# A shorter opening, row norms on VectorE, merged copies and stores from GpSimd in a spectral block with its gradients

## The chip, the cores and the metric

One core of one Trainium2 chip runs the whole program in one launch. Times are device microseconds (us), medians over several executions. TensorE does the matmuls, VectorE, ScalarE and GpSimd the elementwise work, and SyncE issues most transfers. A ratio below is the mean time of one kernel's fast runs over that of the other's of the same rounds, so it is not quite the ratio of the medians quoted beside it; under 1 is faster.

## The reference, cut to what matters

```python
mod = (silu(c) @ w_mod).reshape(1, 6, 1, -1)      # sa, ca, ga, sb, cb, gb
h = layernorm(x) * (1 + ca) + sa
x = x + ga * irfft2(rfft2(h) * (w_r + 1j * w_i))  # a 2-D filter over 2048 x 512
h = layernorm(x) * (1 + cb) + sb
x = x + gb * (relu(h @ w1 + b1)**2 @ w2 + b2)     # 512 -> 1792 -> 512
return x, gradients of all inputs for grad_out
```

The transforms are matmuls with tables of sines that the kernel computes on the chip. `grad_out @ w2^T` depends on no earlier result but the gate `gb`, so its 224 matmuls of 512 columns can be done at any time before the feed-forward part; the kernel uses them as **filler** for TensorE's gaps. Some names that follow: a *fold* adds and subtracts mirrored quarters of a row before it is transformed; the *condition* is c; *scale row* and *gate row* are the rows 1 + ca and gb of `mod`, and the *gate column* (gb2x) is twice gb, turned; psA, psB, psC, psG and the like are tiles in PSUM, TensorE's output memory.

## The kernel before

The filler is placed by a scheduler at low priority (`LATE`), wherever TensorE would otherwise stand:

```python
def back_products(b):                       # b: one of four blocks of 512 rows
    if b > 1:
        scale_g(b)                          # g * 2 gb, VectorE
    with Priority(tc, LATE):
        for fc in range(NFC):               # 14
            ps = mmps.tile([P, SB], FP32, name="mm")
            for dc in range(4):
                nc.tensor.matmul(ps, lhsT=w2T[...], rhs=gT[b][:, :, dc, :], ...)
            with tc.high_priority():
                if fc % 3 == 0:
                    nc.vector.tensor_copy(out=gaT[b][:, fc, :], in_=ps)
                else:
                    nc.scalar.copy(out=gaT[b][:, fc, :], in_=ps)
```

The filter (w_r, w_i) is loaded into eight tiles Z by GpSimd and stored at once, in padded form, for the backward pass; later the complex product of the forward pass overwrites Z in place:

```python
for gi in range(8):
    load_w(gi)                                       # GpSimd queue
    nc.sync.dma_start(wz_dram[:, gi], Z[gi])         # SyncE queue
...
def ew_f(gi, X):                                     # after row transform of group gi
    K["cmul"] = cmul(nc, ew, X, Z[gi], Z[gi][:, :, 0, 0:DF], Z[gi][:, :, 1, 0:DF], False)
    nc.sync.dma_start(xs_dram[:, gi], X)
```

## Time and profile before

| what | value |
|---|---|
| time, first three runs | 433.97 us (431.92 to 434.96) |
| TensorE busy | 398.7 us, 92% of the span |
| VectorE, ScalarE, GpSimd busy | 82%, 59%, 9% |
| last fold of the first stage ends | 40.4 us |
| products of the backward pass that accumulate for long ("gp products") begin | 157.2 us |

For comparing kernels whose stages shift, I cut the first 157 us of the kernel before anew, at events instead of round times: first transform matmul; start of the last fold; first matmul of the table products (psG); first copy of the inverse transform (Tsb); first feed-forward product; first gp product. The busy times of these stretches (columns: stretch, its length, then busy us and instructions of TensorE, weight loads, VectorE, ScalarE, GpSimd; then granted TensorE clock, DMA share, GB/s):

```profile
0.00:14.50 14.50, 4.44 (x14) 1.35 (x14) 9.72 (x54) 6.75 (x12) 9.83 (x54) 1.00 0.97 240
14.50:39.70 25.20, 22.84 (x120) 12.35 (x121) 23.11 (x62) 19.11 (x46) 13.33 (x28) 1.00 0.98 263
39.70:80.00 40.30, 38.02 (x265) 21.22 (x265) 32.33 (x108) 36.04 (x66) 17.62 (x31) 1.00 0.96 264
80.00:93.30 13.30, 13.27 (x121) 8.69 (x121) 10.60 (x20) 7.89 (x15) 0.00 (x0) 1.00 0.83 285
93.30:114.70 21.40, 19.51 (x125) 9.73 (x124) 18.50 (x44) 18.67 (x36) 0.00 (x0) 1.00 0.70 157
114.70:157.20 42.50, 41.29 (x187) 18.06 (x187) 31.43 (x65) 21.26 (x38) 0.00 (x0) 1.00 0.67 218
```

The difference of length and first busy figure in each line is TensorE's idle time: 10.1 us in the opening, 2.4 in A, 2.3 in tables and row transform (B), 0.0 in the table products (C), 1.9 in D, 1.2 in the feed-forward part. The sum is 17.8 us.

### The profile page before, as it was taken

Reading aid. Unit: us, or ns where it says so; the run is one execution under the profiler, and the core shown is the slowest. Engines: PE = TensorE matmul, PEld = TensorE weight load, DVE = VectorE, ACT = ScalarE, POOL = GpSimd, SP = SyncE. Lnnn points to the kernel's source line nnn. Section 1 sums busy time; section 2 is a strip of 40 time slices with the busy share of each in tenths; the row PEclk is TensorE's granted clock in tenths of the full one; section 3 lists DMA queues with packets and bytes.
Section 4 is the critical chain, followed back from the end, with each engine's and each line's share of the span. In section 5 each row is a group of like instructions: output and inputs, shape, how many; then the busy total and the mean of one; then the engine's idle time right before and its main releaser. Section 6 shows DMA issues by size and latency. Waiting matters only on the chain.

```text
span 432.7 us, 7098 instructions
## 1 busy us (share of the span) xinstructions
PE 398.7 (92%) x2353; PEld 196.1 (45%) x2375; DVE 353.7 (82%) x864; ACT 256.1 (59%) x487; POOL 40.9 (9%) x114
## 2 busy tenths in 40 slices
PE   2789999999899999999999999999999799995996
PEld 0344446654344444443444344455555464441332
DVE  6889768959995588969897998929577967989796
ACT  5578699679881286348536765465438374545231
POOL 7447930000000000000000000000000000000000
PEclk9999999999999999999999999999999999998899
DMA  9998899969595379779965997997995599999994
GB/s 237 222 293 278 223 282 273 318 222 188 177 360 191 121 127 329 186 162 226 276 189 158 210 330 271 245 244 217 263 300 160 166 245 257 255 257 255 247 246 137
DMA packets 147147, 101.11 MB, mean 234 GB/s; under 512 B 98945, under 2 KB 131590, under 8 KB 146726
## 3 DMA queue, kind: packets, MB, share of 16 engines
q1 hardware_dynamic: 145458, 98.01, 84.6%
q0 software_dynamic: 1088, 2.11, 2.1%
q10 hardware_dynamic: 564, 0.53, 0.4%
q8 instruction: 19, 0.31, 0.3%
q14 instruction: 18, 0.15, 0.1%
HBM read 35.44 MB, written 41.60 MB: 178 GB/s over the span
## 4 chain that ended last, share of the span: by engine, by line
PE 35%; DVE 25%; ACT 14%; DMA 12%; SPq 5%; issue 5%; POOL 2%; ACTq 0%; DVEq 0%
PE og L901 10%; PE mm L872 8%; PE mm L707 5%; PE mm L1173 4%; DMA out_dram<-gW 2%; PE psG L346 2%; ACT gab L712 2%; DVE gm_junk L470 2%; SPq L1168 2%; DMA n<-n_dram 2%; DMA out_dram<-gw 1%; DVE jk L1258 1%; ACT AE L329 1%; DMA y<-gx_dram 1%; DMA out_dram<-x 1%
## 5 line engine op out<-in xcount | busy, mean ns | idle before, releaser
L707 PE MATMUL mm<-gT,w2T 128*128 128x512 bf16 x224 | 57.8, 383 | 3.0 <-ACT gab L712 3.0
L1173 PE MATMUL mm<-g_sb,hn 128*128 128x512 bf16 x217 | 52.8, 394 | 3.3 <-DVE gw L1176 2.9
L872 PE MATMUL mm<-h2T,w 128*128 128x512 bf16 x224 | 53.4, 378 | 1.6 <-ACT r L874 1.4
L1104 PE MATMUL mm<-gab,h_sb 128*128 128x448 bf16 x256 | 51.4, 352 | 0.8 <-ACT gw L1108 0.8
L901 PE MATMUL og<-w1T,gab 128*128 128x512 bf16 x218 | 49.9, 379 | 1.0 <-DVE o L966 0.8
L901 PE MATMUL og<-w,h 128*128 128x512 bf16 x217 | 49.1, 379 | 0.3
L874 ACT ACTIVATE r<-mm,b1col 128x512 bf16<-128x512 f32 x56 | 37.0, 685 | 6.1 <-PE mm L872 3.3
L1173 PEld LDWEIGHTS <-hn 128*128 128x128 bf16 x224 | 21.6, 100 | 30.5 <-issue 8.2
L1104 PEld LDWEIGHTS <-h_sb 128*128 128x128 bf16 x256 | 24.6, 98 | 22.3 <-issue 1.7
L872 PEld LDWEIGHTS <-w 128*128 128x128 bf16 x224 | 21.1, 97 | 30.0 <-issue 8.3
L901 PEld LDWEIGHTS <-h 128*128 128x128 bf16 x224 | 21.8, 98 | 26.1 <-issue 0.9
L901 PEld LDWEIGHTS <-gab 128*128 128x128 bf16 x224 | 21.6, 98 | 25.9 <-issue 1.4
L707 PEld LDWEIGHTS <-w2T 128*128 128x128 bf16 x224 | 21.2, 98 | 22.4 <-issue 6.4
L914 ACT CAST G<-og 128x512 bf16<-128x512 f32 x16 | 9.2, 580 | 28.1 <-PE og L901 28.1
L876 DVE TENSOR_TENSOR h<-r 128x1024 bf16<-128x1024 bf16 x28 | 19.2, 687 | 4.8 <-ACT r L874 4.8
L1253 ACT ACTIVATE gs<-gn,inv 128x512 bf16<-128x512 bf16 x16 | 11.4, 716 | 18.6 <-DVE gn L1251 18.6
L712 ACT CAST gab<-mm 128x512 bf16<-128x512 f32 x36 | 21.4, 600 | 1.7 <-PE mm L707 1.5
L1108 ACT CAST gw<-mm 128x448 bf16<-128x448 f32 x16 | 8.7, 544 | 22.1 <-DMA out_dram<-gw 12.6
L418 DVE TENSOR_TENSOR p<-Z,G 128x1028 bf16<-128x1028 bf16 x8 | 5.6, 697 | 18.7 <-ACT G L313 10.1
L710 DVE CAST gab<-mm 128x512 bf16<-128x512 f32 x20 | 13.8, 688 | 7.3 <-PE mm L707 7.1
L377 ACT ACTIVATE Tsb<-psT 128x512 bf16<-128x512 f32 x32 | 18.5, 604 | 1.8 <-PE psT L375 1.5
L880 DVE TENSOR_TENSOR gab<-r,gab 128x1024 bf16<-128x1024 bf16 x28 | 19.2, 684 | 0.0
(289 smaller groups left out, 779.7 us busy)
## 6 DMA issues: line engine op xcount, KB each, us to landing
h_dram<-h SPq DMA_DIRECT2D x28, 256.0 KB, 3.6
gh_dram<-gab SPq DMA_DIRECT2D x28, 256.0 KB, 4.3
w<-in_B_w_dram SPq DMA_DIRECT2D x2, 1792.0 KB, 8.8
wmc<-in_w_mod_dram SPq DMA_DIRECT2D x12, 256.0 KB, 4.7
out_dram<-gwm SPq DMA_DIRECT2D x12, 256.0 KB, 3.3
wz_dram<-Z SPq DMA_DIRECT2D x8, 258.0 KB, 3.1
xs_dram<-Xs SPq DMA_DIRECT2D x8, 258.0 KB, 3.0
Z<-wz_dram SPq DMA_DIRECT2D x8, 258.0 KB, 4.1
```

Of the source, the lines that this page charges most:

```text
L377: nc.scalar.activation(Tsb, ps, AF.Copy, scale=EF_S)
L707: nc.tensor.matmul(ps, lhsT=w2T[:, dc, fc * P:(fc + 1) * P], rhs=gT[b][:, :, dc, :], start=(dc == 0), stop=(dc == 3))
L710: nc.vector.tensor_copy(out=gaT[b][:, fc, :], in_=ps)
L712: nc.scalar.copy(out=gaT[b][:, fc, :], in_=ps)
L872: nc.tensor.matmul(ps, lhsT=w1[:, dc, (fc + i) * P:(fc + i + 1) * P], rhs=h2T[b][:, :, dc, :], start=(dc == 0), stop=(dc == 3))
L874: nc.scalar.activation(r[:, i, :], ps, AF.Relu, bias=b1col[:, fc + i:fc + i + 1])
L876: nc.vector.tensor_tensor(h2, r, r, op=ALU.mult)
L880: K["gh"] = nc.vector.tensor_tensor(gh, r, gh, op=ALU.mult).ins
L901: nc.tensor.matmul(ps, lhsT=lhs(fc), rhs=rhs[:, fc, :], start=(fc == 0), stop=(fc == NFC - 1))
L1104: nc.tensor.matmul(ps[:, 0:W4], lhsT=h2_sb[:, t, dc * P:(dc + 1) * P], rhs=ghn[t // 4][:, t % 4, fs], start=(t == 0), stop=(t == NT - 1))
L1173: nc.tensor.matmul(ps, lhsT=hns[fc][:, t, :], rhs=g_sb[:, t, :], start=(t == 0), stop=(t == NT - 1))
L1253: nc.scalar.activation(gs[:, i, :], gn[:, i, :], AF.Copy, scale=inv1[:, t + i:t + i + 1], accum_out=rr[:, i, 0:1])
```

## The change

Its intent, in its own few words: a short opening chain; norms on VectorE and product copies of two blocks on ScalarE; one copy per transform row; filter and table stores from GpSimd. The core of the diff (cuts marked with ...):

```diff
-    nc.scalar.dma_start(vrow[0:4, :], c...)          # one tile with the bias rows
-    nc.scalar.dma_start(vrow[4:4 + NFC, :], B_b1...)
+    nc.scalar.dma_start(crow, c...)                  # the condition alone
 ...
-        scb = p0.tile([P, 4, P], BF16, name="scb")
-        for dc in range(4):
-            nc.scalar.activation(scb[:, dc, :], pv[:, dc:dc + 1].broadcast_to([P, P]), AF.Copy, scale=sigcol[:, dc:dc + 1])
+        scb = p0.tile([P, 4], BF16, name="scb")
+        nc.vector.tensor_tensor(scb, pv[:, 0:4], sigcol, op=ALU.mult)
 ...
     with tc.high_priority():
         mod_row(1)
-        mod_row(5)                                   # gate row, gate column: now after the first fold
 ...
+    def load_g(b):
+        if b == 2:                                   # third block: into the fourth's product tile
+            gT.append(gaT[3][:, NFC - 4:NFC, :]...)
+        else:
+            gT.append(w2gp.tile([P, TB, 4, P], BF16, name="gT", bufs=2))
+        nc.sync.dma_start(gT[b]..., transpose=True)
 ...
-            if t == 0 or (t + j) % 4 == 3:
-                nc.vector.tensor_scalar(row, row, i1, nb, op0=ALU.mult, op1=ALU.add)
-            else:
-                K["scaled"] = nc.scalar.activation(row, row, AF.Identity, bias=nb, scale=i1).ins
+            nc.vector.tensor_scalar(row, row, i1, nb, op0=ALU.mult, op1=ALU.add)
 ...
+    load_g(2)
     for gi in range(8):
+        if gi == 4:
+            load_g(3)
         load_w(gi)
-        nc.sync.dma_start(wz_dram[:, gi], Z[gi])
+    for gi in range(8):
+        nc.gpsimd.dma_start(wz_dram[:, gi], Z[gi])
 ...
-                    if fc % 3 == 0:
+                    if b > 1 and fc % 2 == 0:
                         nc.vector.tensor_copy(out=gaT[b][:, fc, :], in_=ps)
 ...
-        nc.sync.dma_start(LG_dram[:, 4 * q:4 * q + 4], K["LG"][:, 4 * q:4 * q + 4])
+        nc.gpsimd.dma_start(LG_dram[:, 4 * q:4 * q + 4], K["LG"][:, 4 * q:4 * q + 4])
```

Besides, the two half-row transform copies and the two AE copies of a group become one each, with the blocks in another order in PSUM.

## The prediction

> **What bounds the kernel now.** I read the page first, then the busy times by stage, then the chain of waits of the first 17 us and the groups of instructions up to 130 us, because nearly all of the edit lies there.
>
> From the page, the busy tenths of 40 slices of 10.8 us:
>
> ```profile
> PE   2789999999899999999999999999999799995996
> DVE  6889768959995588969897998929577967989796
> ACT  5578699679881286348536765465438374545231
> ```
>
> TensorE is busy nearly everywhere except at the opening (2, 7) and late (7 and 5 of the last ten slices). A busy slice is not a full one, so I count matmuls. The stages that the change touches, from the busy times by stage (columns: stretch, its length, busy us and instructions of TensorE, weight loads, VectorE, ScalarE, GpSimd, then clock, DMA share, GB/s):
>
> ```profile
> 14.50:42.00 27.50, 25.08 (x133) 13.63 (x135) 25.41 (x74) 21.01 (x51) 15.63 (x32) 1.00 1.00 263
> 42.00:62.30 20.30, 19.42 (x130) 9.86 (x129) 14.81 (x64) 16.69 (x28) 15.32 (x27) 1.00 0.85 240
> 62.30:80.00 17.70, 16.36 (x124) 10.08 (x123) 15.22 (x32) 17.44 (x34) 0.00 (x0) 1.00 1.06 291
> 89.20:116.00 26.80, 24.66 (x152) 11.85 (x151) 21.53 (x50) 22.73 (x44) 0.00 (x0) 1.00 0.66 163
> ```
>
> Call these A (row norms and first transform), B1 (filter tables), B2 (row transform, 8 groups), D (inverse transform and second norms); between B2 and D lie 9 us (C) in which TensorE is full. In A VectorE sets the pace (25.4 of 27.5 us), in B2 ScalarE (17.4 of 17.7), in D VectorE from about 96 us on. The 224 matmuls of the gated back product (L707) are filler in all of them: 66 run in A, 49 in B1, 32 in B2, 76 in D. From 130 us to 280 us TensorE is the bound: 47 matmuls of 512 columns fall in the 10 us from 130, so 0.213 us each, back to back. Whatever is won before 130 us therefore shifts all the rest, and is kept.
>
> The opening, from the chain of waits (start, us, what):
>
> ```profile
> 1.32 4.29 DMA vrow<-in_B_b_dram
> ...
> 6.15 1.28 ACT L105
> ...
> 13.15 0.48 ACT modb L603
> ...
> 13.98 0.04 DVE gb2x L616
> ...
> 14.05 0.42 DVE fold_u L250
> ```
>
> The 18-row load waits for the bias to land at 5.62 us, then sigmoid, then a table load, then the scale row. VectorE has the first scaled rows ready at 12.2 us but stands in front of the gate column (gb2x), which needs a second row of products, so the first fold starts only at 14.05 and the first transform matmul at 14.53.
>
> The costs I use, from the groups up to 130 us (mean ns is the second number after the bar):
>
> ```profile
> L712 ACT CAST gab<-mm 128x512 bf16<-128x512 f32 x36 | 21.4, 600 | 1.7 <-PE mm L707 1.5
> L710 DVE CAST gab<-mm 128x512 bf16<-128x512 f32 x20 | 13.8, 688 | 7.3 <-PE mm L707 7.1
> L645 ACT ACTIVATE x_sb<-x_sb,l_nb,inv 128x512 bf16<-128x512 bf16 x10 | 8.1, 818 | 5.2 <-POOL l_nb L637 5.2
> L643 DVE TENSOR_SCALAR x_sb<-x_sb,inv,l_nb 128x512 bf16<-128x512 bf16 x6 | 2.4, 417 | 0.4 <-POOL l_nb L637 0.4
> L289 ACT CAST utcs<-psA 128x256 bf16<-128x256 f32 x32 | 9.7, 391 | 2.8 <-PE psA L287 2.8
> L329 ACT ACTIVATE AE<-psB 128x512 bf16<-128x512 f32 x8 | 6.5, 818 | 0.9 <-PE psB L323 0.9
> ```
>
> Neighbours overlap, so in a row an instruction takes less than its duration. By the distance of starts in the timeline: product copy 0.47 us on ScalarE and 0.60 on VectorE, norm 0.71 and 0.31, half-row transform copy 0.30, AE copy 0.59.
>
> **What the Trainium skill says.** "VectorE: DVE Perf Modes", section "The perf-mode tier table", puts bf16 tensor_scalar in SBUF in the fastest tier and says that PSUM sources drop a tier. The trace agrees: 417 ns for a norm, 688 ns for a copy of the same 512 columns out of PSUM. So norms belong on VectorE and PSUM copies on ScalarE. "ScalarE: Activation LUTs", section "What ACT_TABLE_LOAD costs", gives a switch of tables 1283 ns, ACTIVATE 0.833 ns an element plus a fixed part, and 93 ns for each pointer operand; the table load here is 1.28 us, and the norm with two pointer operands takes 818 ns where the plain copy takes 600. "DMA: Bandwidth & Descriptors", section "Issuing engines are not separate DMA queues", says that another issuing engine saves only sequencer time; in this trace the queue of SyncE waits 10.0 us in all, 8 times, for the filter loads before it can store them.
>
> **The change part by part.**
> Opening: the condition row alone is awaited, not the bias; the sigmoid times condition is one small VectorE product in place of four ScalarE fills (1.12 us together); the first two rows are loaded as 256 KB instead of 512; the gate row and gb2x move behind the first fold. Estimate: condition landed near 4 us, scb near 6, four matmuls of the scale row at the cold spacing of 0.43 us done near 8.5, its copy 0.69, product h 0.6, fold 0.7: first transform matmul near 10.5 instead of 14.5. GpSimd agrees: its index work ends near 7.3 us, the power chain takes 1.0, norms 0.7, so h can start near 9.4.
> Stage A: VectorE loses 6 product copies (6 x 0.60 = 3.6 us, and some 1.9 us of waits for them) and gains 10 norms (10 x 0.31 = 3.1). ScalarE loses 10 x 0.71 = 7.1 us and has one 512-column copy per row instead of two of 256: 16 x (0.60 - 0.47) = 2.1 us. VectorE has some 30 us to do from 5.2 us on, so with 2 us of waits A could end at 37 instead of 40.4 (last fold). But rows 8 to 11 are issued at 13.45 us, and the loads of rows take 7.1 to 8.0 us to land. The old kernel reached row 8 at 20.9 us; the new one would be there at 19 and must wait to about 21. From rows 12 (landing near 27.5) VectorE has some 10 us left: last fold at 37.4. I take 3.0 us won.
> B1 and B2: all product copies of blocks 0 and 1 go to ScalarE, and the other two blocks are split half and half, so ScalarE has 42 instead of 36 in all. By the order of instructions ScalarE has 10 instead of 7 in B1 and 11 instead of 6 in B2, VectorE 1 instead of 7 over both. One AE copy of 1024 elements instead of two of 512 saves the fixed part, some 0.15 us, in each group. B1 is paced by the filter tables on VectorE and ScalarE in turn; without VectorE's waits for product copies (about 3 us) it shrinks from 20 to about 17 to 18 us. In B2 ScalarE has 7 x 1.05 (AE; one instead of two groups are done before) + 16 x 0.47 + 11 x 0.47 = 20 us instead of 17.4. Together 39 us, as before: nothing won, nothing lost.
> D: fewer fillers were placed in A (38 instead of 66), so 101 instead of 76 remain: 25 x 0.213 = 5.3 us of TensorE. Up to the last transpose of the first block VectorE has 7 copies in place of 5, but less of the next block's norms (about 2.4 us) in front, so that point comes about 2 us sooner after the start of D. Then 31 fillers follow in one go (6.6 us), in whose shadow the next block's norms are done. After them the first feed-forward products, which lose some 2.3 us now between 116 and 130, run unbroken. Net for D: about 1.4 us lost.
> The rest: the AE copies in the second row transform (280 to 320 us) get shorter, but TensorE has 10.0 of 10 us there: nothing. Stores from GpSimd free SyncE's queue, but the tables land in time already: nothing.
> Sum: -3.0 + 0 + 1.4 = -1.6 us by my counting. The waits that I could not count (ScalarE's 5.2 us of waits for l_nb, 3.0 us of TensorE's for the product copies) can only shrink in part, for which I give another 2.2 us. 434.0 - 3.8 = 430.2.
>
> **The rivals.**
> One: the start is the whole story, and the 4 us of the opening and about as much again in A and B1 are kept, since TensorE has the same work in all and the gaps merely go. For it: TensorE needs about 85 us up to 116, so 31 us are gaps, 14.5 of them at the opening. Against it: filler pushed back has to be done somewhere. It gives 424 to 427.
> Two: ScalarE becomes the bound. It is already 17.4 of 17.7 us busy in B2 and gets 5 more copies there. If the AE copy saves nothing and B1 does not shrink, B grows by 2 to 3 us and D by 1.4, and the change is worth nothing or costs 1 us: 433 to 436. For it speaks the count; against it, that ScalarE has 3.6 us idle in B1.
> Three: the load of rows 8 to 15 binds A more than I think, for the transposes hold SyncE's queue (6.9 us for the first). Then A ends at 39, and the time is about 432.
>
> **Range and chances.** The sum of parts has an uncertainty of 1.5 us in A, 1.5 in B, 2 in D; runs of one kernel scatter by 3 us. Hence 425.8 to 434.2. Faster by 2% means under 425.3, only rival one at its best: 0.09. Slower by 2% needs 442.7: 0.02. Within 2%: 0.89.
>
> **What would show it.** First transform matmul at 10.5 us and last fold near 37.4; a wait of VectorE for rows 8 to 11; ScalarE full in B2, and B as long as before; 31 product matmuls without a break before the first feed-forward product; the first product with w2 begun at about 126 instead of 129.9 us, and the same distance from there to the end. I am wrong if VectorE does not wait for rows, if D keeps its length, or if the late part, with its DMA-filled slices, does not move along with its start.

## More of the kernel before

Runs of this kernel scatter by some 4 us around their median on one chip, so I also compare points in time inside the profiles. Each kernel has one profile only.

The gradient blocks g are loaded transposed, four of them into two buffers, so that the load of the third block has to wait until the products of the first are done:

```python
for b in range(NB):
    gT.append(w2gp.tile([P, TB, 4, P], BF16, name="gT", bufs=2))
    nc.sync.dma_start(gT[b]..., g_view[...], transpose=True)
```

## The result

The changed kernel takes 439.35 us (438.37 to 440.12, 4 runs), beside 434.46 (431.92 to 434.96) for the kernel before. The ratio is 1.0123, 95% interval 1.0076 to 1.0171. It is slower by about 5 us where I had said 4 us faster, and it lies outside my range. All runs compared here were fast.

From the page of the changed kernel, TensorE's and ScalarE's tenths and the granted clock in 40 slices of 11 us:

```profile
PE   2879989689999999999999999999999899995996
...
ACT  4367999258775069338824765463357466445231
...
PEclk9999999899999999999999999999999999997899
```

Slice 8 (76.7 to 87.6 us) is new: TensorE at 6 tenths and its clock at 8 tenths. The busy times by stage, cut at the same events as before:

```profile
0.00:11.40 11.40, 2.41 (x7) 0.73 (x7) 7.97 (x48) 4.44 (x6) 8.17 (x49) 1.00 0.88 235
11.40:35.20 23.80, 19.55 (x100) 10.39 (x101) 23.80 (x74) 12.60 (x24) 14.22 (x32) 1.00 1.07 269
35.20:81.00 45.80, 39.39 (x270) 21.60 (x270) 27.59 (x99) 39.06 (x62) 24.04 (x42) 1.00 1.15 236
81.00:95.80 14.80, 13.81 (x117) 8.59 (x116) 12.15 (x22) 6.48 (x12) 0.54 (x1) 0.88 0.86 314
95.80:123.20 27.40, 25.86 (x156) 12.39 (x157) 24.35 (x58) 21.16 (x41) 0.00 (x0) 1.00 0.52 125
123.20:164.20 41.00, 40.48 (x186) 17.87 (x191) 28.89 (x57) 20.21 (x35) 0.00 (x0) 1.00 0.71 225
```

Length less busy gives TensorE's idle time: 9.0, 4.2, 6.4, 1.0, 1.5 and 0.5 us, 22.7 in all instead of 17.8. (TensorE also counts as busy while it runs at a lower clock, so a loss of clock is not in this sum.) Read as differences of length: the opening won 3.1 us, A another 1.4; B lost 5.5, C 1.5, D 6.0; the feed-forward part won 1.5. That sums to the 7.0 us by which the gp products begin later (164.2 instead of 157.2). From there to the end the profile of the changed kernel is 1.5 us shorter (274.0 against 275.5), and no run here shows why.

Four readings of the changed kernel name the losses.

**The opening is bound by another chain now.** From the chain of waits up to 14 us (start, us, what):

```profile
7.87 0.73 POOL inv L406
8.62 0.16 DVE l_nb L645
8.79 0.60 DVE l_st L637
9.39 0.64 DVE x_sb L653 x2
10.14 0.18 DVE l_mv L638
10.32 0.57 DVE h L657
```

The condition row is no longer on it; GpSimd's index work and its power instruction are. VectorE fits the next row's statistics (l_st, 0.60 us) in before the norms, so product h starts at 10.32, not at the 9.4 I had estimated, and the first transform matmul at 11.43.

**A is paced by VectorE without a pause, and B by a store.** From the waits of 11 to 135 us (engine and line, what it waited for, us in all, times, longest):

```profile
DVE Z L420 <- DMA wz_dram<-Z: 8.3, 1, 8.3
...
PE psA L287 <- DVE fold_u L251: 5.2, 3, 2.9
PE mm L741 <- DVE gab L744: 4.1, 2, 3.8
...
ACT Tsb L377 <- DMA xs_dram<-Xs: 2.1, 1, 2.1
```

The complex product overwrites Z (L420), so it must wait until Z's store has read it. GpSimd issues the eight stores only at 65.44 us, behind all 34 filter loads in its own queue, while the product is ready to overwrite Z near 61; in the kernel before, SyncE issued the first store at 45.45. The issues, changed kernel first (start, us, engine, line, operation, names, count):

```profile
65.44 4.33 POOL L701 DMA_DIRECT2D wz_dram<-Z  x8
```

```profile
45.45 6.68 SPq L667 DMA_DIRECT2D wz_dram<-Z  x4
```

VectorE stands 8.3 us, its later work slips, and the product copy behind it (gab, L744) is what TensorE then waits for. TensorE's queue around that point (start, us, engine, line, operation, names, shapes, count, idle time before):

```profile
76.01 0.59 PE L741 MATMUL mm<-gab,w2T 128*128 128x512 bf16 x2
80.42 0.59 PE L741 MATMUL mm<-gab,w2T 128*128 128x512 bf16 x2 [3.82 <-DVE gab L744]
80.96 2.39 PE L346 MATMUL psG<-LG,Z 128*128 128x256 bf16 x13
```

**The gap is paid twice.** The same stretch in slices of 2 us (columns as above; the number before the last two is the granted clock):

```profile
76.00:78.00 2.00, 0.60 (x4) 0.19 (x2) 1.97 (x5) 1.28 (x3) 0.00 (x0) 1.00 1.07 416
78.00:80.00 2.00, 0.00 (x0) 0.00 (x0) 2.00 (x7) 0.00 (x0) 0.60 (x1) 1.00 1.23 125
80.00:82.00 2.00, 1.57 (x10) 1.00 (x10) 2.00 (x5) 0.00 (x0) 0.07 (x1) 0.90 1.16 369
82.00:84.00 2.00, 2.00 (x18) 1.16 (x16) 2.00 (x5) 0.59 (x1) 0.47 (x1) 0.50 1.03 397
84.00:86.00 2.00, 2.00 (x33) 1.21 (x33) 2.00 (x6) 0.91 (x2) 0.00 (x0) 0.75 1.06 373
```

TensorE stands from 76.6 to 80.4 us; a little over 1 us after it resumes, its clock falls to half for some 3.4 us (0.4, 2.0 and 1.0 us by the last three lines) while it is full of work. The first 16 table products take 3.03 us there and 1.92 in the kernel before. The Trainium skill, "TensorE: Matmul & The Clock Gate", section "What's actually happening", says that the array's clock falls to half after an idle window of about 3.4 us and comes back after as long a busy one. The trace agrees in kind and in size: the wait is 3.8 us, the half clock some 3.4, and (1 - 0.88) x 14.8 us of C is 1.8 us of full clock lost. Apart from the cold spacing of the scale row, nothing in my prediction counted the clock; in the clock column the old kernel has 1.00 in all six stretches. That column misses the start, though: it reads 1.00 there, but the first transform products start 0.21 us apart, and 0.11 us apart later. The old kernel reaches the quicker pace at 18.1 us; the changed one is still slow at 17.7 and quick at its next transforms, at 20.8.

**The copies.** From the groups up to 130 us, shapes kept apart (busy us, mean ns, then idle before and releaser):

```profile
L746 ACT CAST gab<-mm 128x512 bf16<-128x512 f32 x42 | 25.3, 613 | 6.1 <-PE mm L741 5.8
...
L330 ACT ACTIVATE AE<-psB 128x1024 bf16<-128x1024 f32 x8 | 11.9, 1490 | 0.2 <-PE psB L325 0.2
...
L289 ACT CAST utcs<-psA 128x512 bf16<-128x512 f32 x16 | 8.9, 590 | 12.0 <-PE psA L288 11.9
...
L653 DVE TENSOR_SCALAR x_sb<-x_sb,inv,l_nb 128x512 bf16<-128x512 bf16 x16 | 5.9, 400 | 0.0
```

The norms cost what was worked out. The merged AE copy takes 1490 ns on average where one of the two old ones took 818, and by the distance of starts it occupies ScalarE for 1.18 us, exactly twice the old 0.59. ScalarE waits 11.9 us for transforms in A: it has been relieved of more than it needed, while VectorE has 23.8 us of work in 23.8.

So there were several candidate causes: the stores from GpSimd (S), the filler that left A (F: 38 instead of 66 matmuls before A's end), the last store of the row transform Xs, which lies behind the 1792 KB load of w1 in SyncE's queue and for which the first inverse copy waits 2.1 us (T), and the moved norms (N).

### The profile page after: what moved, and what is told of

The parts are those of the page before. It is cut to its first block, busy times and chain, and to the rows that moved or that the text cites.

```text
span 438.2 us, 7046 instructions
## 1 busy us (share of the span) xinstructions
PE 400.4 (91%) x2354; PEld 196.5 (45%) x2376; DVE 352.7 (80%) x870; ACT 250.1 (57%) x447; POOL 47.1 (11%) x124
## 4 chain that ended last, share of the span: by engine, by line
PE 37%; DVE 29%; ACT 15%; DMA 10%; issue 5%; SPq 2%; POOL 2%; ACTq 0%; DVEq 0%; POOLq 0%
PE og L935 8%; PE mm L1138 7%; PE mm L906 5%; PE mm L741 4%; DMA xs_dram<-Xs 4%; PE mm L1207 4%; ACT AE L330 3%; DMA n<-n_dram 3%; ACT gab L746 2%; DVE gm_junk L470 2%; SPq L1202 2%; ACT v L963 2%; PE psC L311 2%; ACT n2rows L969 1%; DVE jk L1292 1%
## 5 line engine op out<-in xcount | busy, mean ns | idle before, releaser
L741 PE MATMUL mm<-gT,w2T 128*128 128x512 bf16 x168 | 43.8, 386 | 2.8 <-ACT gab L746 2.4
L1138 PEld LDWEIGHTS <-h_sb 128*128 128x128 bf16 x256 | 24.6, 98 | 21.4 <-issue 0.8
L741 PEld LDWEIGHTS <-w2T 128*128 128x128 bf16 x224 | 21.1, 99 | 27.3 <-issue 12.2
L746 ACT CAST gab<-mm 128x512 bf16<-128x512 f32 x42 | 25.3, 613 | 6.1 <-PE mm L741 5.8
L330 ACT ACTIVATE AE<-psB 128x1024 bf16<-128x1024 f32 x16 | 22.7, 1417 | 1.9 <-PE psB L325 1.8
L1287 ACT ACTIVATE gs<-gn,inv 128x512 bf16<-128x512 bf16 x16 | 11.4, 716 | 16.8 <-DVE gn L1285 16.8
L1142 ACT CAST gw<-mm 128x448 bf16<-128x448 f32 x16 | 8.6, 540 | 21.4 <-DMA out_dram<-gw 12.1
## 6 DMA issues: line engine op xcount, KB each, us to landing
w<-in_B_w_dram SPq DMA_DIRECT2D x2, 1792.0 KB, 13.2
```

The source lines that it names most:

```text
L330: nc.scalar.activation(dst, ps.rearrange("p r (s e f) -> p (r s) e f", s=2, e=2), AF.Copy, scale=EF_S)
L741: nc.tensor.matmul(ps, lhsT=w2T[:, dc, fc * P:(fc + 1) * P], rhs=gT[b][:, :, dc, :], start=(dc == 0), stop=(dc == 3))
L1138: nc.tensor.matmul(ps[:, 0:W4], lhsT=h2_sb[:, t, dc * P:(dc + 1) * P], rhs=ghn[t // 4][:, t % 4, fs], start=(t == 0), stop=(t == NT - 1))
L1287: nc.scalar.activation(gs[:, i, :], gn[:, i, :], AF.Copy, scale=inv1[:, t + i:t + i + 1], accum_out=rr[:, i, 0:1])
```

## The experiments

Each was run beside the kernel before on the same chip. "gp" is the start of the gp products in its profile; the kernel before has 157.2, the changed one 164.2.

### e1_stores_back

```diff
-    for gi in range(8):
-        nc.gpsimd.dma_start(wz_dram[:, gi], Z[gi])
+        nc.sync.dma_start(wz_dram[:, gi], Z[gi])      # in the loop of loads again; LG stores likewise
```

> The changed kernel, but the filter and table stores issued from SyncE again, each filter store right behind its load. Theory S (the stores): GpSimd issues all eight filter stores only after all filter loads, and the complex product that overwrites the filter has to wait for its store; VectorE's 8.3 us wait for the filter store should fall under 1 us, the first table product of the inverse transform should start near 77 us instead of 81.0, and the time should fall by 4 to 6 us against the changed kernel, to 433.5 to 435.5. Theory F (filler): the loss is the back-product matmuls that are no longer placed in the opening stage and must be done later; the store wait is merely hidden idle time, so the time stays within 1 us of the changed kernel, 438.5 to 440.

Measured: 442.17 us, ratio 1.0146 (1.0083 to 1.0209), gp 166.4. The wait before the complex product is gone and the table products start at 78.3, as expected. But with the stores back on SyncE that queue runs later, the w1 load is issued at 87.05, and ScalarE waits 5.5 us for the Xs store before the first Tsb copy (96.9 us). The time part of theory S fell: taking this wait away handed the time to the next one.

### e2_old_pool_stores

The same edit in the other direction, on the kernel before: both stores from GpSimd, behind all loads.

> The kernel before, with only the filter and table stores moved to GpSimd. Theory S: the complex products wait for the filter stores, which leave after about 59 us, while the first product wants to write at about 65: a wait of 1 to 4 us on VectorE, and 1 to 4 us more than before, 435 to 438. Theory F: no change, 433.5 to 435.

Measured: 435.97 us, ratio 1.0007 (0.9934 to 1.008), gp 158.9. The old kernel bears the stores from GpSimd within the noise, and VectorE has no wait for them. There the filter loads are issued from 37.9 to 58.5 us, the stores at 59.06, and the first product that overwrites Z stands at 65.3. In the changed kernel the loads begin sooner and are drawn out (33.1 to 64.9 us, with 12.2 us in which GpSimd waits for earlier loads), and the product comes sooner: the margin of 6 us has become a deficit.

### e3_lagged_pool_stores

```diff
     for gi in range(8):
         load_w(gi)
-    for gi in range(8):
-        nc.gpsimd.dma_start(wz_dram[:, gi], Z[gi])
+        if gi >= 2:
+            nc.gpsimd.dma_start(wz_dram[:, gi - 2], Z[gi - 2])
+    for gi in (6, 7):
+        nc.gpsimd.dma_start(wz_dram[:, gi], Z[gi])
```

> The changed kernel with the filter stores still on GpSimd, but each one issued two loads behind its own load instead of all at the end (table stores on GpSimd too). Theory S as order within the queue: VectorE's wait for the filter store nearly vanishes and the time equals that of the run with the stores on SyncE within 1.5 us, 433.5 to 436.5. If it is the GpSimd path itself (slower stores) and not the order: half or less of the gain, 437 to 439. Theory F: 438.5 to 440.

Three of its four runs fell in the slow state, so it has no usable time. Its (slow) profile shows the table products at 78.3 and Tsb waiting 3.7 us for the Xs store at 93.1.

### e4_filler_first

```diff
-        with Priority(tc, LATE):
+        with Priority(tc, LATE if b > 0 else -3000):   # products of block 0 as early as possible; on top of e1
```

> As the run with the stores back on SyncE, and in addition the first block's back products get a priority above the row transforms, so that 68 of the 224 fillers stand before the end of the row transforms instead of 38 (the kernel before: 66) and 15 instead of 31 behind the last transpose. Theory F: less TensorE time is left idle in the opening stage, so 1.5 to 4 us less than the run with the stores back: 430.5 to 433. Rival: the fillers in front hold the row transforms up by as much as they save later: within 1 us of the run with the stores back.

Measured: 438.6 us, ratio 1.004 (0.9965 to 1.0115). With 68 instead of 38 fillers before A's end, A ends 8 us later (43.4), and yet the kernel is 1% faster than e1 beside the same runs of before (1.004 and 1.0146, three and four fast runs, none of which overlap). By these few runs a late end of A with filler in it beats an early one without. Its profile, from which the 43.4 us comes, was slow and is left out of the table below.

### e5_old_w1_late, e6_new_w1_late

```diff
-            nc.sync.dma_start(xs_dram[:, gi], X)
+            K["xs"] = nc.sync.dma_start(xs_dram[:, gi], X).ins
 ...
-        nc.sync.dma_start(w1, w1_view)
+        with tc.issue_after(K["xs"]):
+            nc.sync.dma_start(w1, w1_view)
```

> The kernel before, with one change: the load of the feed-forward weight w1 (1792 KB) is issued behind the last store of the row transform on SyncE's queue instead of in front of it. Theory T (a hidden floor: the first inverse copy, Tsb, cannot begin until the stores of the row transform have landed, and the last of them queues behind the w1 load): the store lands about 2 us sooner, Tsb begins near 91 instead of 93.3 us, and 1.5 to 2.5 us are kept to the end: ratio 0.994 to 0.997. Rival (the floor is not there in the old kernel; the 80 to 89 us stretch of table products sets Tsb): Tsb stays at 93 and the ratio is 1.000 within 0.2%.

> The changed kernel, with the w1 load behind the last store of the row transform and nothing else. The filter stores still come from GpSimd behind all loads, so the table products still start near 81 us and end near 91. Theory T: Tsb no longer waits for the store, begins 1 to 3 us sooner (93 to 94.5 instead of 95.8), and the time falls by about as much: 437 on a chip where the changed kernel has 439. Rival (only the filler decides): Tsb moves but the 31 back-product matmuls in front of the feed-forward products take the gain: ratio against before stays 1.012.

On the old kernel: 435.15 us, ratio 1.002 (0.9998 to 1.0042), gp 157.1, Tsb at 93.1 as before. Theory T fell there: the old kernel has no hidden floor behind the w1 load. On the changed kernel: 439.05 us, ratio 1.0089 (1.0055 to 1.0123), Tsb at 93.9 instead of 95.8, gp 162.6. The wait exists in the changed kernel and is worth 1.6 us there in the profile; in time the two ratios (1.0089 and 1.0123) have overlapping intervals.

### e7_new_lag_w1_late

Edits of e3 and e6 together: both waits for stores mended.

> The changed kernel, GpSimd's filter stores issued two loads behind their loads (no wait before the complex product), and the w1 load behind the last store of the row transform. Theory T (both waits added up to what the opening had won): the table products start near 78 us, Tsb near 89.5, the first feed-forward product 3 to 4 us sooner than in the changed kernel (near 119 to 120), and the time is 434.5 to 436.5: equal to before within 0.5%. Rival (filler alone): Tsb comes sooner, but the first product with w2 stays at 131 to 133 us and the ratio at 1.010 or above.

Measured: 437.53 us, ratio 1.0049 (1.0023 to 1.0076), gp 158.9. The table products start at 78.0 and Tsb at 90.4, 3 us ahead of the old kernel. The first feed-forward product nevertheless comes at 117.9, 3.2 behind it: D takes 27.5 us instead of 21.4, with the filler in it that was not done before. Mending the stores thus brings back 5.3 of the 7.0 us (1.6 of them by the w1 load alone, e6, so 3.7 with the order of the filter stores). That the rest is the filler, as theory F has it, is argued from D, and the shares don't add up: e14 below, which only puts the load of the third g block and with it most of the filler back, recovers 4.1 us, and both mends together (e15) only 3.8. D of this kernel (columns as before):

```profile
90.40:117.90 27.50, 25.99 (x157) 12.38 (x157) 24.35 (x58) 21.22 (x41) 0.00 (x0) 1.00 0.64 163
```

Its A shows the clock again (slices of 2 us):

```profile
22.00:24.00 2.00, 0.16 (x2) 0.15 (x3) 2.00 (x6) 0.44 (x1) 0.99 (x3) 1.00 0.79 259
24.00:26.00 2.00, 1.36 (x9) 0.72 (x8) 2.00 (x7) 1.40 (x3) 1.55 (x3) 0.64 1.18 257
26.00:28.00 2.00, 2.00 (x6) 0.76 (x5) 2.00 (x9) 1.02 (x3) 0.70 (x4) 0.51 1.00 222
```

TensorE has nothing to do while VectorE prepares the next rows; the longest single wait is 2.18 us, and half clock follows.

### e8_filler_lag_w1

Edits of e3, e4 and e6 together.

> As the run before it, and in addition the back-product matmuls of the first block are placed as early as they can be in the row-norm stage (68 instead of 38 before its end), which makes the first transforms end later (near 43 instead of 35 us). Theory F (TensorE is the bound up to 280 us, so gaps in the first stage left unfilled are lost): the first product with w2 comes 1 to 3 us sooner than in the run before it, near 127 to 130, and the time is 431 to 434, the best of all so far. Rival (the first stage's end matters more than its filler): 436 or more.

Measured: 435.86 us, ratio 1.0012 (0.9987 to 1.0037), gp 157.6. Stores mended and filler kept, the changed kernel is as fast as the old one within 0.4%. The expected 431 to 434 was missed: 4.1 us of A remain idle: VectorE is busy for 30.0 of A's 30.8 us, and TensorE's longest gap there (2.18 us, before 23.85) has no filler in it.

### e9_old_norms_copies

The kernel before with the norms and the split of product copies of the change, nothing else.

> The kernel before with two parts of the change alone: all norms of the first stage on VectorE, and the product copies of the first two blocks on ScalarE, half of the others on VectorE. Filler placed before the end of the first stage: 64 matmuls, against 66 before. Theory F (what counts is TensorE's idle time before the long stage that begins with the gp products, 17.8 us in the old kernel): the two parts trade engines, VectorE sets the pace of the first stage either way, so idle time stays within 1 us and the first gp product at 156.5 to 158; ratio 0.998 to 1.002. Rival N (the moves themselves overload VectorE in the first stage, as its 100% in the changed kernel suggests): the gp products begin 2 us or more later and the ratio is above 1.004.

Measured: 432.9 us, ratio 0.9934 (0.9906 to 0.9962), gp 155.7. Both theories were wrong about it: this part wins. TensorE's idle time in A falls from 2.4 to 0.6 us and A gets 3.1 us shorter (22.1), with 64 fillers still in it.

### e10_opening_alone

The changed kernel with norms, product copies and AE copies as before, stores and w1 mended.

> The changed kernel with its opening, but norms, product copies and the AE copy as in the kernel before, and with both mends (filter stores two loads behind, w1 load behind the last row-transform store). So the short opening nearly alone; filler before the end of the first stage is 38, as in the changed kernel. Theory F: the first transform matmul comes 3.1 us sooner, but TensorE's idle time before it falls by only about 1 us, since the second scale row and the gate column moved behind it; 28 fillers fewer in the first stage mean as much idle time there; the gp products begin at 157 to 160 and the ratio is 1.000 to 1.007. Rival N (the norms on VectorE are what costs): without them the opening's gain is kept, gp products begin near 155, ratio 0.993 to 0.996.

Measured: 436.78 us, ratio 1.0041 (1.001 to 1.0071), gp 159.0. As theory F has it: the first transform matmul is 3.2 us sooner, and the time is lost again behind it (idle in A 4.5 us, D 27.5 us). Rival N falls together with e9. In spite of its name, this kernel still holds the change's load of the third g block, so it doesn't show that the opening drives the filler out of A; e13 tests that.

### e11_old_one_ae_copy

```diff
-            nc.scalar.activation(dst[0], src[:, 0], AF.Copy, scale=EF_S)
-            nc.scalar.activation(dst[1], src[:, 1], AF.Copy, scale=EF_S)
+            nc.scalar.activation(dst, ps.rearrange("p r (s e f) -> p (r s) e f", s=2, e=2), AF.Copy, scale=EF_S)
```

> The kernel before with one ScalarE copy of 1024 elements in each row-transform group in place of two of 512, and the block order that it needs. My prediction credited it 0.15 us a group. By the trace of the changed kernel one copy occupies ScalarE 1.18 us, the two together 1.18: so nothing is saved, the distance from the first psC product to the last stays 24.6 us within 0.5, ratio 1.000 within 0.3%. Rival (the fixed part is saved, 8 times 0.15 in the first and as much in the second row transform): 1 us less there, ratio 0.997.

Measured: 434.62 us, ratio 0.9981 (0.9958 to 1.0004), gp 158.7. From the first to the last psC product it is 24.6 us, as before. The one copy in this kernel (duration min, median, max in ns, then first and last start):

```profile
L330 ACT ACTIVATE AE<-psB x8: 1325/1395/1453, 53.1 to 76.2; 128x1024 bf16<-128x1024 f32 x8
```

Nothing is saved in the first row transform; a gain of up to 0.4% elsewhere is not excluded by the interval.

### e12_more_filler

```diff
-        with Priority(tc, LATE if b > 0 else -3000):
+        with Priority(tc, LATE if b > 1 else -3000):   # on top of e8
```

> As e8, but the fillers of two blocks instead of one are placed early: 112 before the end of the first stage, none left between the last transpose of the first block and the feed-forward products. Theory F: TensorE's gaps in the first stage (4.1 us in e8) shrink, since VectorE paces its transforms anyway and TensorE waits there for folds; gp products begin at 154 to 157, ratio 0.992 to 0.999. Rival E (what ends late in the first stage pushes tables and row transform back, and TensorE idles there in its place): gp products at 158 or later, ratio 1.002 or above.

Measured: 439.29 us, ratio 1.0099 (1.007 to 1.0127), gp 161.6. Rival E was right: with 112 fillers before A's end by the order of instructions (88 of them begin before the last fold does), A ends at 46.5, its own idle time does not shrink (4.8 us), and D has none left to fill its gaps (3.8 us idle). Filler is a stock; it can be spent too early as well as too late.

### e13_old_third_block

By the order of instructions, 66 fillers before A's end become 38 through one edit alone, tried on the old kernel: the load of the third g block. The opening, which I had blamed, leaves them where they were.

```diff
-    for b in range(NB):
-        gT.append(w2gp.tile([P, TB, 4, P], BF16, name="gT", bufs=2))
+    def load_g(b):
+        if b == 2:
+            gT.append(gaT[3][:, NFC - 4:NFC, :]...)
+        else:
+            gT.append(w2gp.tile([P, TB, 4, P], BF16, name="gT", bufs=2))
 ...
+    load_g(2)                                # before the filter loads
 ...
+        if gi == 4:
+            load_g(3)
```

> The kernel before with one edit of the change alone: the load of the third g block goes into the product tile of the fourth block, and the third and fourth loads are issued where the change issues them. The order of instructions has 38 fillers before the end of the first stage, as in the changed kernel, against 66. Theory L (this edit moves the fillers, and moved fillers are lost time): the first stage ends sooner (36 to 38 us) but the gp products begin at 159 to 162 instead of 157.2; ratio 1.005 to 1.012. Rival (moving fillers is neutral: TensorE does them later in gaps that were there anyway): gp products at 157 within 1, ratio 1.000 within 0.3%.

Measured: 441.42 us, ratio 1.021 (1.0157 to 1.0264), gp 166.6. This one edit alone costs the old kernel 9 us, more than expected. D becomes 27.4 us long, as in the changed kernel. In addition, C becomes 18.8 us long; its stretch and its wait:

```profile
79.60:98.40 18.80, 14.28 (x117) 8.89 (x118) 10.76 (x19) 7.05 (x13) 0.00 (x0) 0.82 0.98 324
```

```profile
PE psF L359 <- DMA LG<-LF_dram: 4.5, 1, 4.5
```

The edit also shifts SyncE's queue: its first LG transpose starts at 70.24 us instead of 58.12, behind filter stores that wait for their loads there. That second loss is absent from the changed kernel, whose filter stores do not stand in SyncE's queue. So the parts of the change seem to belong together, the stores from GpSimd making room for the earlier g loads; no run tests this by itself. e13 does not separate the filler's share from the queue's by time; by stage it is 6.0 us in D and 5.5 in C.

### e14_new_third_block_back, e15_new_all_mended

The reverse edit on the changed kernel, and on e7.

> The changed kernel with the third and fourth g blocks loaded as in the kernel before, and nothing else undone. 58 fillers before the end of the first stage instead of 38, 209 instead of 193 before the last transpose of the first block. The filter stores still come late from GpSimd and the last row-transform store still lies behind the w1 load. Theory L: the gp products begin 2 to 5 us sooner than in the changed kernel, at 159 to 162; ratio against before 1.002 to 1.008 (1.0123 for the changed kernel). Rival (the waits for stores are all): 164 and 1.012.

> The changed kernel with the third and fourth g blocks loaded as before, filter stores two loads behind, w1 load behind the last row-transform store. Theory L: all three causes are gone and what the short opening and the norms win is kept: gp products at 153.5 to 156, ratio 0.988 to 0.996. Rival (the opening is worth nothing to TensorE, which had work in it): as the norms and copies alone on the old kernel, 155.7 to 157.5, ratio 0.994 to 1.001.

Measured: e14 438.09 us, ratio 1.011 (1.0052 to 1.0168), gp 160.1; e15 439.1 us, ratio 1.011 (1.0041 to 1.0179), gp 160.4. The gp products of e14 come 4.1 us sooner than in the changed kernel, within what theory L said; but the ratio of 1.011 is hardly under the changed kernel's 1.0123, with four fast runs each, so a gain in time is not shown. e15 missed both expectations. D shrank to 23.9 us, but C grew to 18.3, because the g load now waits for its buffer again and VectorE stands before scaling it. From the waits of e15 between 74 and 100 us:

```profile
DVE gT L623 <- DMA gT<-in_grad_out_dram: 5.5, 1, 5.5
PEld L359 <- DVE Z L420: 4.3, 2, 2.2
PE psF L359 <- DVE Z L420: 3.9, 2, 2.0
```

Such a wait is what the third-block edit avoids. In the old kernel it does not show: the last g load is issued at 67.18 us there, at 69.98 in e15, and the scaling behind it comes at 75.3 without a wait, at 79.57 in e15 after 5.5 us of waiting.

### e16_norms_short_chain

e9, and of the opening only the condition row, the small VectorE product and the 256 KB first load; gate row and gate column stay where they were.

> The old kernel with the norms on VectorE and the product copies of the change (as e9: 155.7 us, 0.9934), and of the opening only the short condition chain: condition row alone awaited, the sigmoid product on VectorE, first two rows loaded first. Gate row, gate column and fillers stay where they were (65 before the end of the first stage). Theory L: first transform matmul 1.5 to 3 us sooner than 14.0, gp products 1 to 2 us sooner than in e9, near 154; ratio 0.988 to 0.992. Rival: VectorE sets the first stage by its sum of work and the start is lost in waits for rows 8 to 11: as e9.

Measured: 430.98 us beside 433.14 for the old kernel, ratio 0.9953 (0.9929 to 0.9977), gp 154.0, as theory L expected in the profile; the ratio is no better than e9's. The first transform matmul hardly moves (13.9 us), because the gate column still stands in VectorE's way. Its first four stretches:

```profile
0.00:13.90 13.90, 4.42 (x15) 1.47 (x15) 9.61 (x54) 5.03 (x7) 9.62 (x54) 1.00 0.96 250
13.90:36.20 22.30, 22.06 (x120) 12.36 (x121) 22.30 (x68) 16.31 (x43) 12.95 (x28) 1.00 1.04 273
36.20:77.70 41.50, 38.49 (x267) 21.20 (x265) 30.05 (x104) 37.52 (x69) 17.75 (x31) 1.00 1.05 253
77.70:91.40 13.70, 13.68 (x123) 8.91 (x124) 12.12 (x22) 7.30 (x13) 0.00 (x0) 1.00 0.90 327
```

Idle time is 9.5, 0.2, 3.0 and 0.0 us here, and 15.2 in all up to the gp products, the least of all kernels. VectorE is as full in A as in the changed kernel, but TensorE has 120 matmuls there instead of 100.

### e17_new_filler_kept, e18_new_scalar_stores

e15 with the filler of block 0 early (as e4); and the changed kernel with the third block back and filter stores from ScalarE in the loop of loads.

> As e15 (the changed kernel with the g blocks loaded as before, filter stores two loads behind, w1 load behind the last row-transform store), and the products of the first block placed early: 63 fillers before the end of the first stage, 111 before the first row-transform product. Idle time of TensorE before the gp products is what counts: 9.0 in the opening (9.5 in e16), 1 to 4 in the first stage, 3 in tables and row transform, at most 1 in the table products. Theory O (the opening is worth 0.5 to 1 us of TensorE time at most, since the old opening had matmuls in it): gp products at 153.5 to 156.5, ratio 0.993 to 0.998, like e9 and e16. Rival P (the whole 2.5 us by which the first transform comes sooner than in e16 are kept): 151 to 152.5, ratio 0.985 to 0.990.

> The changed kernel with the g blocks loaded as before and the filter stores issued from ScalarE in the order of the loads, instead of from GpSimd behind all loads. 58 fillers before the end of the first stage, 112 before the first row-transform product, all 224 before the last transpose of the first block. Theory O: no wait for a store before the complex products, gp products at 154 to 157 if ScalarE is not held by its stores, ratio 0.993 to 1.000. Rival Q (ScalarE stands in front of a store until the loads have landed, as SyncE did for 15 us in e16): row transform 3 us or more later, ratio 1.004 or above.

Measured: e17 438.4 us, ratio 1.005 (1.0022 to 1.0079), gp 158.0, outside both expectations: the g load's wait is still 3.2 us, C is 18.2 us long with its clock at 0.91. e18 446.43 us, ratio 1.0245 (1.0195 to 1.0294), gp 167.9, as rival Q: ScalarE stands 11.3 us in front of a store until its filter loads have landed.

### All of them side by side

e3 and e4 are left out, since their profiles are slow. "Idle" is length less TensorE's busy time, summed from 0 to gp; the clock is the lowest of the six stretches.

| kernel | first transform | Tsb | gp | idle | lowest clock | ratio |
|---|---|---|---|---|---|---|
| before | 14.5 | 93.3 | 157.2 | 17.8 | 1.00 | 1 |
| changed | 11.4 | 95.8 | 164.2 | 22.7 | 0.88 | 1.0123 |
| e1 | 11.3 | 96.9 | 166.4 | 25.2 | 0.93 | 1.0146 |
| e2 | 14.5 | 94.9 | 158.9 | 18.7 | 1.00 | 1.0007 |
| e5 | 14.4 | 93.1 | 157.1 | 17.5 | 1.00 | 1.002 |
| e6 | 11.4 | 93.9 | 162.6 | 21.7 | 0.86 | 1.0089 |
| e7 | 11.4 | 90.4 | 158.9 | 19.7 | 0.93 | 1.0049 |
| e8 | 11.4 | 92.8 | 157.6 | 17.0 | 0.94 | 1.0012 |
| e9 | 14.0 | 92.7 | 155.7 | 16.6 | 1.00 | 0.9934 |
| e10 | 11.3 | 89.5 | 159.0 | 19.5 | 0.93 | 1.0041 |
| e11 | 14.2 | 94.7 | 158.7 | 18.0 | 1.00 | 0.9981 |
| e12 | 11.3 | 99.2 | 161.6 | 20.3 | 0.96 | 1.0099 |
| e13 | 14.9 | 98.4 | 166.6 | 24.3 | 0.82 | 1.021 |
| e14 | 11.4 | 95.0 | 160.1 | 18.5 | 0.91 | 1.011 |
| e15 | 11.3 | 95.2 | 160.4 | 18.5 | 0.91 | 1.011 |
| e16 | 13.9 | 91.4 | 154.0 | 15.2 | 1.00 | 0.9953 |
| e17 | 11.4 | 94.9 | 158.0 | 16.7 | 0.91 | 1.005 |
| e18 | 11.4 | 105.3 | 167.9 | 27.7 | 0.91 | 1.0245 |

The start of the first transform says nothing about the time: 11.3 goes with 1.0146 and 13.9 with 0.9953. Neither does Tsb: the two earliest, e10 and e7, are slower than before. Gp less idle time is TensorE's busy time, by definition; it lies between 138.8 (e16) and 142.3 us (e13), with 139.4 before and 141.5 in the changed kernel. A fallen clock can lengthen it but does not decide it alone: e11, whose clock never fell, has 140.7, and e7, whose clock did, 139.3. So idle time explains most of gp, not all. The order by gp is nearly the order by ratio.

## Why the prediction was wrong

**"The rest: ... the tables land in time already: nothing."** This step failed most. I asked whether the stores' data come in time for somebody who reads them, and not who has to wait before overwriting what they read. VectorE waited 8.3 us for that, TensorE 3.8, its clock fell to half, and the Xs store behind the w1 load took over as the next wait. With both mended (e7) the gp products come 5.3 us sooner, and the ratio is 1.0049 instead of 1.0123.

**"The opening", and "A ... 3.0 us won".** The direction was right and the size was not what counts. The first transform came at 11.4 instead of the predicted 10.5, and the last fold ended at 36.0 instead of 37.4; VectorE waited for loads of rows only 0.2 us in all, where I had taken rows 8 to 11 to bind. So A ended 4.4 us sooner (36.0 instead of 40.4), not 3.0. But TensorE's idle time up to the last fold went from 12.4 to 13.2 us: the old opening held two scale rows (4.44 us of TensorE work), the new one holds one (2.41), and A was emptied of filler. "Whatever is won before 130 us therefore shifts all the rest, and is kept" is true of TensorE's time only, not of the end of a stage. The first product with w2, by which I wanted to see it, came at 132.8 us instead of 126; the kernel before has 129.4 (the 129.9 of the prediction is misread).

**"D: ... net about 1.4 us lost".** The mechanism was right and the term was mis-sized. 31 fillers did stand before the first feed-forward product (115.5 to 123.2 us), interrupted only by four products of the inverse transform. D grew by 6.0 us where I had 5.3 less 2, and the later products got back 1.5 where I had 2.3: net 4.5. (My own terms add up to 1.0, not to the 1.4 that I wrote.) Of the "2 us sooner" for the last transpose of the first block 0.8 was there (19.7 us after the start of D, 20.5 before; in e7 19.8).

**Why the filler left A.** The prediction took 38 for given and, by its place in the text, for a result of the shorter A. The order of instructions, taken for each edit alone, shows that the third g block does it, and the profiles agree: 64 fillers begin before the last fold in the kernel before, 36 in the changed kernel and in e13, 52 in e14. That the move costs is shown on the old kernel (e13); on the changed one it shows in gp (e14), not in time. I had passed over this edit because no word of the change named it.

**"B ... together 39 us, as before".** It took 45.8 us instead of 40.3 from the last fold to the table products, and even with the stores mended (e7) 42.7. The AE copy's 0.15 us a group was not there (e11), as rival two supposed, and those 2.4 us more in e7 lie in the 2 to 3 us that it gave for B.

**The clock** was in no step. In the profiles, a wait of TensorE of 2 to 4 us was often followed by 3 us or more at half clock (e7, e8 and the changed kernel). Every kernel of the table with a clock under 1.00 has at least 3.8 us of idle time in A or D, 6.4 in B or 1.9 in C; the kernels that never dip have at most 2.4 in A or D, 3.2 in B and 1.0 in C. These limits are read off afterwards from one profile each; they describe the table and are no rule.

**The "further 2.2 us given"** for waits that I could not count was a wish; the uncounted waits grew.

Of the rivals, one ("gaps merely go") failed for the reason it named against itself. Two gave the nearest range, 433 to 436, with B about right, but without the waits for stores and the real size of D. Three (row loads) did not occur.

**What stays open.** Whether the full opening is worth anything once no queue holds the stages behind it: e15 and e17 were both held in C by the g load. By the sum of idle time it would be 0.5 us (9.0 in the opening against 9.5 in e16), an estimate from these two profiles. How the loss divides between stores and filler is open too, since e7, e14 and e15 do not add up. Why the scheduler places fewer fillers after the third-block edit is not shown; only that it does. What makes the last 100 us differ by some 4 us between profiles of similar kernels (95.0 from the last matmul of the second row transform in e8, 98.8 before) is only indicated by the granted clock there, 0.98 against 0.96.

The best kernels found are e9 and e16, 0.5 to 0.7% faster than the kernel before and, through it, about 1.7% faster than the changed one (from the ratios 1.0123 and 0.9953, not measured side by side). They keep the norms and copies, and of the opening at most the condition chain.

## What to carry to other kernels

Where free filler exists, add up the bound engine's idle time over all stages and judge every edit by that sum; an earlier end of one stage proves nothing. Before moving a store to another queue, ask who overwrites its source and what stands in front of it in the new queue, then ask the same of the transfers that it no longer delays. Read every hunk of a diff, and compare the order of instructions for each edit alone.

## What the Trainium skill lacked or had wrong

- "TensorE: Matmul & The Clock Gate", "What's actually happening": it gives an idle window of about 3.4 us. A later section of the page, "A second HAM failure mode: psum-queue depth-cycling", says that frequent short idles between groups of matmuls also make the clock swing, but gives no duration for them. In e7 the longest single wait in A was 2.18 us, in e8 too, and half clock followed in both (0.51 in e7 from 26 to 28 us); in the changed kernel a wait of 2.04 us at the same place was followed by none. So gaps well under the window, with light work around them, sometimes cost; what decides is not shown here.
- "ScalarE: Activation LUTs", "What ACT_TABLE_LOAD costs": 186 ns and 0.833 ns an element would be 1039 ns for the merged AE copy (an estimate from the section's figures); it took 1490 ns on average in the changed kernel and 1395 (median) in e11, and occupied the engine for 1.18 us. The same 512 columns out of PSUM took 590 ns in the transform copy and 818 in the old AE copy, which interleaves its output. The section has no term for such a layout, and merging saved nothing in e11.
- "DMA: Bandwidth & Descriptors", "Issuing engines are not separate DMA queues": it says that another issuing engine only saves sequencer time. Here the engine, with the place in its order, decided when the stores were issued at all (from 65.44 instead of 45.45 us), and with that an 8.3 us wait of VectorE, and on ScalarE (e18) an 11.3 us one; two loads behind their own load on GpSimd again (e7), VectorE did not wait for them. The order of issue on each engine would deserve a sentence there.
